# A pair's split queries and keys go to their matmul operands by way of DRAM, and two-block pieces are transposed in one transfer

## The chip, the cores and the metric

The kernel runs on one core of one Trainium2 chip. The metric is the device time of one execution in microseconds, median of the runs shown. The core has five engines with an instruction stream each: TensorE (PE, with its weight loads as PEld), VectorE (DVE), ScalarE (ACT), GpSimd (POOL) and SyncE (SP). In this kernel SP issues every DMA; its rows are marked SPq. Each stream runs in order: an instruction that waits holds up everything behind it on its engine.

## The reference

Attention with a decay bias, and behind it a two-layer network with an ELU in the middle, all in 32-bit floats:

```
scores = (q @ k.T) / sqrt(64)                     # 8 batches x 8 heads, 576 x 576, head size 64
cum    = cumsum(max(s, 0))                        # along the sequence
scores = where(causal, -1e9, scores + min(cum[key] - cum[query], 0))
attn   = exp(scores - rowmax);  attn /= rowsum + 1e-9
x      = attn @ v                                 # 4608 tokens x 512
h      = x @ w_in                                 # 512 -> 2048
out    = where(h > 0, h, exp(min(h, 0)) - 1) @ w_out   # 2048 -> 512
```

## The kernel before

**Work.** A "pair" is two heads of one batch; a "piece" is a batch with a range of its 128-query blocks. Three kinds of piece come in this order: batches 0 to 2 with blocks 0 and 1 ("low", computed in 32 bits, 12 units); then batch 3 with blocks 0 and 1 and batches 4 to 7 whole (20 pairs, named with `_None` in the profile because their preparation hangs on a unit without a head number); then blocks 2 and 3 of batches 0 to 3 (16 "late" pairs). The 18 chunks of 256 tokens of the network follow the pieces and fill TensorE between the attention steps.

**A pair's operands.** Outside the low stage every 32-bit number is split into two 16-bit floats, a high and a low part, and products are sums of 16-bit matmuls. `prepare_pair` loads a pair's keys (`stk`) and queries (`stq`), two transfers for keys and two or four for queries, the first head in partitions 0 to 63 and the second in 64 to 127. It takes their largest value (`peak`, L601 and L604), makes a scale from it (`pk`, L939 to L941), and splits them into `kp` and `qp` (L408 to L410 high, L960 or L956 and L957 low). Then `spread` copies the parts into the operand tile `set`, where both heads lie side by side and a column holds 64 numbers of one part above 64 of another: two transfers (one a head) for each of the six places `kh`, `kh2`, `qh`, `qh2`, `kl`, `ql`, so twelve, and a thirteenth brings the decay rows (`set<-aux_dram`). There are two sets, used in turn. Then come the scores (L1040), the masked minimum (L1043), the exponential (L1048).

**Weights times values.** `halved` scales a block's exponentials and splits them into `p16` tiles (L1093, L1095 or L1097 high, L1101 or L1087 and L1088 low); one DMA transpose per block (`turned_load`, L389) brings them into `T`; `weighing` multiplies by the values (L1209) when all transposes of both heads are there, and the result goes to `x_dram`. For a late pair both heads use the same two `p16` tiles, so that the second head's splitting waits until the first head's transposes have read them. The first 64 queries of a pair are one small extra unit (`psh_None`, `tr_None`, `vs_None`); its 64 value rows have a transfer of their own (`stv`), into one of the three `st` buffers that the keys and queries use as well.

**Network.** `load_x` loads a chunk (`xc<-x_dram`), one transfer per 128 channels and row range; then come the split (`xh`, `xl`), the first layer (L1383), the ELU (L1395 to L1422) and the second layer (L1440).

**Order.** No order is written by hand. `Plan` gets every step with an estimated cost per engine that could do it, and places, one by one, the step that can start first (then the one of highest priority) on its engine's stream. A plain transfer costs SP 430 ns in it (`SP_COST`), a transpose 1250 ns, and data are taken to land 1800 ns (`LAG`) plus bytes / 225 (`RATE`) after their turn in the transfer queue. The resulting order is fixed; at run time each engine only waits for semaphores.

Of the kernel before, what the change touches and what calls it, by code (L numbers as in the profile page):

```python
# [17 lines left out]
P = 128  # L18
# [9 lines left out]
N_ST, N_A, N_AV, N_H, N_IO, N_G, N_X, N_T, N_V = 3, 2, 1, 3, 3, 1, 1, 2, 4  # L28
# [17 lines left out]
SP_COST = 430.0  # L46
# [12 lines left out]
class Buf:  # L59
# [15 lines left out]
    @property  # L75
    def v(self):
        if self.tile is None:
            self.tile = self.make()
        return self.tile

# [5 lines left out]
class Plan:  # L86
# [41 lines left out]
    def op(self, prio, ways, reads=(), writes=(), late=()):  # L128
# [5 lines left out]
        for accesses, write in ((reads, False), (writes, True)):  # L134
            for a in accesses:
                b, part = a if isinstance(a, tuple) else (a, None)
                if not b.parts and b not in o.bufs:

                    o.new.append((b, self.place(b)))
                    b.first = o  # L140
# [195 lines left out]
def kernel(  # L336
# [46 lines left out]
    def load(prio, dst, src, reads, writes, nbytes, late=(), lag=LAG):  # L383
        return op(prio, [("SP", SP_COST, lambda: nc.sync.dma_start(dst(), src()), lag, nbytes)],  # L384
                  reads, writes, late)

    def turned_load(prio, units, dst, src, reads, writes):

        op(prio, [("SP", 1250.0, lambda: nc.sync.dma_start_transpose(dst(), src()), LAG,  # L389
                   units * P * P * 2)], reads, writes)  # L390
# [119 lines left out]
    Q1, Q2, K1, K2 = range(4)  # L510
# [61 lines left out]
    pair_sets = [plan.buf(const, [P, 4, 2, S], F16, "set_0")]  # L572

# [6 lines left out]
    all_tops = [plan.buf(const, [P, P], F32, f"tops_{m}") for m in range(3)]  # L580
# [11 lines left out]
    junk = const.tile([P, 2 * (NQ + 1) * D], BF16, name="junk")  # L592
# [22 lines left out]
    def scales_of(prio, spans, dst):  # L615

        n = len(spans)
        kind = 1 if dst == 0 else 2 * (dst >= C_LOW)
# [119 lines left out]

    def prepare_low(u):
# [4 lines left out]
        u.q = plan.buf(sb, [P, 2 * LOW], F32, f"ql_{u.tag}", tag="qs", bufs=2)  # L744
# [23 lines left out]
    def scoring_low(u):  # L768
        prio = u.prio
        sm = plan.buf(sb, [P, 1 + 2 * CUT], F32, f"sml_{u.tag}", tag="sm", bufs=2)  # L770
        u.first = plan.buf(sb, [P, P], F32, f"pl_{u.tag}", tag=("khs", "vs0")[u.turn])
        u.pp = {}
        tiles = [(u.first, P)]
# [9 lines left out]
        def block(i, h):  # L783
            n = 1 + 2 * i + h
            place = i + CUT * u.turn
            if h == 0:
                pt = pp[place]
            else:
                pt = plan.buf(sb, [P, pd[i]], F32, f"pl{n}_{u.tag}", tag=f"p16_{place}")
# [81 lines left out]
    def group_values(u):  # L871
# [4 lines left out]
        nv = 2 * (u.last + 2)  # L876
        whole = nv - 2 * (u.last < NQ - 1)
        va = plan.buf(sb, [P, NP, nv, D], F32, f"va_{at}", tag=home.key[1])
        for j in range(NP):
            load(prio + j, lambda j=j: va.v[:, j, :whole], lambda j=j: vb[u.b, j, :, 1 : 1 + whole], [],  # L880
                 [(va, (j, "whole"))], P * whole * D * 4)
            for rows in HALF[: nv - whole]:
                load(prio + j, lambda j=j, rows=rows: va.v[rows, j, whole:], lambda j=j: vb[u.b, j, :HB, 1 + whole : 1 + nv],
                     [], [(va, (j, rows.start))], HB * 2 * D * 4)
# [6 lines left out]
        return va, col  # L891

    def pair_values(u, va, col):
# [4 lines left out]
        src = lambda: va.v[:, u.j].rearrange("p (n h) d -> p h n d", h=2)  # L898
# [16 lines left out]
    def prepare_pair(u, o):  # L915
# [6 lines left out]
        kp, qp = (plan.buf(sb, [P, 2, S], F16, f"{m}p_{u.tag}", tag="qs", bufs=2) for m in "kq")  # L922
        for m, rows in enumerate(HALF):
            load(prio, lambda m=m, rows=rows: sk.v[rows, :n], lambda m=m: kT[b, :HB, 2 * j + m, :n], [], [(sk, m)],
                 HB * n * 4)
        for m, rows in enumerate(HALF):
            if c0:
                at = (1 - m) * (w - HB)
                load(prio, lambda rows=rows, at=at: sq.v[rows, at : at + HB],
                     lambda m=m: qT[b, j, :HB, m * HB : (m + 1) * HB], [], [(sq, (m, 0))], HB * HB * 4)  # L930
            load(prio, lambda m=m, rows=rows: sq.v[rows, m * c0 : m * c0 + nb * P].rearrange("d (i t) -> d i t", t=P),
                 lambda m=m: qT[b, j, :HB, P:].rearrange("d (i m t) -> d i m t", m=2, t=P)[
                     :, u.blocks[0] : u.last + 1, m], [], [(sq, (m, 1))], HB * P * nb * 4)
# [15 lines left out]
        def split(m, size, t, src):  # L949

            high, low = (lambda: t.v[:, 0, :size]), (lambda: t.v[:, 1, :size])
            x = lambda: src.v[:, :size]
            scaled(prio, size, high, x, lambda: by(m), [src, (pk, 2)], [(t, 0)])
# [9 lines left out]
            ], [(pk, 2), (t, 0)], [src, (t, 1)])  # L963
# [20 lines left out]
        load(prio, lambda: o.v[HB : HB + 3, K2, :, :n],  # L984
             lambda: aux_dram.v[b * H + 2 * j : b * H + 2 * j + 2, :, :n].rearrange("h m t -> m h t"),
             [aux_dram], [(o, "aux")], n * 12)
        spread(kp, 1, n, top, K2, "kl")
        spread(qp, 1, w, low, Q1, "ql")
# [3 lines left out]
    def prepare(u):  # L992
# [14 lines left out]
        u.vs = plan.buf(sb, [P, 1, 2, D], F32R, f"vs_{u.tag}", tag="vs0")  # L1007
        v_src = lambda: vb[b, j, :, 0:1]
        sv = st_buf(f"stv_{u.tag}")

        def v3():
            return sv.v[:, :D].rearrange("p (n d) -> p n d", d=D)
# [3 lines left out]
        rest(prio, D, lambda: u.vs.v[:, :1, 1], v3,  # L1016
             lambda: u.vs.v[:, :1, 0].bitcast(F32), [sv], [u.vs])
# [51 lines left out]
    def halved(u, i, pt, sm, col):  # L1069

        r, prio = slice(col, col + 1), u.prio
        k, turns = (pw[i] + HB * (i < u.last)) // P, u.turns[i]
        t16 = plan.buf(sb, [P, turns * P], F16, f"p16_{u.tag}_{i}", tag=f"p16_{i + u.step}")

        def whole(t, m):
            v = t.v[:, P:] if i == u.last else t.v
            return v.rearrange("p (k m q) -> p k m q", m=2, q=P)[:, :, m]

        def rest(t, m):
            return t.v[:, m * HB : (m + 1) * HB]  # L1080
# [5 lines left out]
        def scaled_rest(part):  # L1086
            pool.tensor_scalar(own(part), own(part), sm.v[:, r], 1.0, ALU.mult, ALU.mult)  # L1087
            pool.tensor_tensor(part(t16, 1), own(part), part(t16, 0), ALU.subtract)  # L1088

        for part, n in ((whole, k * P), (rest, HB))[: 1 + (i == u.last)]:  # L1090
            high, low = (part, 0), (part, 1)
            op(prio, [
                ("Pool", 160 + 1.04 * n, lambda part=part: pool.tensor_scalar(  # L1093
                    part(t16, 0), own(part), sm.v[:, r], 1.0, ALU.mult, ALU.mult)),
                ("DVE-SB", 220 + 0.7 * n, lambda part=part: dve.tensor_scalar(  # L1095
                    part(t16, 0), own(part), sm.v[:, r], None, ALU.mult)),
                ("ACT", 295 + n / 1.2, lambda part=part: act.activation(  # L1097
                    part(t16, 0), own(part), AF.Copy, scale=sm.v[:, r])),
            ], [sm, (pt, "data"), (pt, "pad")], [(t16, high)])
            op(prio, [  # L1100
                ("DVE-SB", dve_2(n), lambda part=part: dve.scalar_tensor_tensor(  # L1101
                    part(t16, 1), own(part), sm.v[:, r], part(t16, 0), ALU.mult, ALU.subtract)),
                ("Pool", pool_1(n) + pool_2(n), lambda part=part: scaled_rest(part)),
            ], [sm, (pt, "pad"), (t16, high)], [(t16, low), (pt, "data")])
# [504 lines left out]
```

## Time and profile before

| what | value |
|---|---|
| time, median of 3 runs | 1146.38 us (1142.46 to 1148.72) |
| the profiled execution, its own time | 1142.85 us |
| its span, first to last instruction | 1141.0 us |
| mean granted TensorE clock | 0.976 |
| PE / DVE / ACT / POOL busy | 1035.0 / 842.7 / 676.5 / 262.0 us |
| DMA queue, share of 16 engines' span | 58.9% |
| transfers into `set` from `kp` and `qp` | 432 |
| DMA transposes | 208 |

"Busy" counts an engine's own work, so SP, which only issues, has no such number; the length of an issue stands in the rows of its line and in the timeline. A wait row says which engine and line stood idle, what ended the idle time, the sum, the times, and the longest. The profile's stretches here are the low stage and its passage (0 to 150 us), the 20 pairs (about 150 to 750), the 16 late pairs (about 750 to 1050), and a tail of network alone.

### The profile page before, as it was taken

The page shows a single profiled execution, that of the slowest core. Times are in us where ns is not written, and L with a number is a line of the kernel's source. Part 1 is how long each engine was busy: PE and PEld are TensorE (multiplying, and loading weights), DVE is VectorE, ACT ScalarE, POOL GpSimd, SP SyncE. Part 2 cuts the span into 40 slices and gives each one's busy share as a digit, 9 for nine tenths or more (in the row PEclk, how much of TensorE's full clock was granted, in tenths as well). Part 3 has the DMA queues.
Part 4 walks back from the last instruction along what each step waited for, and adds up shares of the span by engine and source line. Part 5 has one row for each costly group of instructions (what it writes and reads, how often), then busy time and mean ns, then how long its engine had stood idle before and what let it go on. Part 6 is the DMA issues. An engine that isn't in the chain of part 4 may idle for free.

```text
span 1141.0 us, 22403 instructions
## 1 busy us (share of the span) xinstructions
PE 1035.0 (91%) x7299; PEld 695.8 (61%) x7299; DVE 842.7 (74%) x2361; ACT 676.5 (59%) x1579; POOL 262.0 (23%) x442
## 2 busy tenths in 40 slices
PE   7999998799899688989899998898999899899998
PEld 6676565566556456656566665565666566566665
DVE  7997997558778687878688876777788687776332
ACT  5887755456556565656566665565566565546343
POOL 6331442121322222222232222111122112200000
PEclk9999999999999889999899999999999999999999
DMA  7897224345656686667666866575575675655200
GB/s 194 270 276 227 58 89 86 94 101 164 142 137 132 154 190 139 125 147 165 142 151 136 194 130 155 118 182 125 134 181 127 135 160 137 140 123 102 50 20 19
DMA packets 304665, 158.41 MB, mean 139 GB/s; under 512 B 218356, under 2 KB 286692, under 8 KB 304548
## 3 DMA queue, kind: packets, MB, share of 16 engines
q1 hardware_dynamic: 304548, 156.98, 58.9%
q8 instruction: 58, 0.95, 0.4%
q14 instruction: 59, 0.48, 0.1%
HBM read 62.80 MB, written 19.24 MB: 72 GB/s over the span
## 4 chain that ended last, share of the span: by engine, by line
PE 35%; DVE 10%; DMA 8%; SPq 6%; issue 4%; ACT 3%; POOL 0%; DVEq 0%; ACTq 0%; POOLq 0%
PE h L1383 15%; PE o L1440 13%; SPq L384 5%; PE sc L1040 3%; PE av L1209 3%; DMA T<-p 2%; DMA stq<-in_qT_dram 2%; DMA x_dram<-x_None 2%; DVE p L1043 2%; DVE p L1101 2%; SPq L389 1%; DVE h L1415 1%; ACT g L1395 1%; DMA va<-in_vb_dram 1%; DMA stq_None<-in_qT_dram 1%
## 5 line engine op out<-in xcount | busy, mean ns | idle before, releaser
L1383 PE MATMUL h<-xh,wp 128*128 128x256 f16 x2176 | 408.3, 276 | 2.5 <-DVE gg L1422 1.7
L1440 PE MATMUL o<-wp,gg 128*128 128x512 f16 x1632 | 398.2, 383 | 4.7 <-DVE gg L1422 2.9
L1383 PEld LDWEIGHTS <-wp 128*128 128x128 f16 x3264 | 321.5, 99 | 74.9 <-issue 3.6
L1383 PE MATMUL h<-xl,wp 128*128 128x256 f16 x1088 | 300.6, 276 | 0.9 <-DVE xl L1359 0.8
L1440 PEld LDWEIGHTS <-gg 128*128 128x128 f16 x1632 | 158.6, 99 | 155.5 <-DVE gg L1422 6.8
L1101 DVE SCALAR_TENSOR_TENSOR p<-p,sm,p 128x512 f16<-128x512 f32 (+3 forms) x268 | 159.1, 618 | 28.7 <-ACT p L1097 24.1
L1048 ACT ACTIVATE p<-p,mn 128x192 f32<-128x192 f32 (+1 forms) x232 | 143.6, 619 | 39.3 <-DVE mn L1043 37.8
L1415 DVE SCALAR_TENSOR_TENSOR h<-g,cs,h 128x512 f32<-128x512 f32 x136 | 102.0, 750 | 55.5 <-ACT g L1402 53.8
L1395 ACT ACTIVATE g<-h,cs 128x512 f32<-128x512 f32 x136 | 92.6, 681 | 82.8 <-PE h L1383 82.5
L1093 POOL TENSOR_SCALAR p<-p,sm 128x512 f16<-128x512 f32 (+3 forms) x96 | 63.9, 670 | 335.5 <-DMA T<-p 113.2
L1040 PE MATMUL sc<-set 128*128 128x288 f16 (+3 forms) x544 | 114.2, 303 | 28.2 <-DVE mn L1043 26.1
L1043 DVE CUSTOM_DVE_ANT_0 p<-sc,maskw 128x192 f32<-128x192 f32 (+1 forms) x232 | 109.3, 480 | 21.4 <-PE sc L1040 17.2
L1419 ACT ACTIVATE gg<-h 128x512 f16<-128x512 f32 x129 | 76.5, 593 | 73.0 <-DVE h L1415 68.4
L1097 ACT ACTIVATE p<-p,sm 128x512 f16<-128x512 f32 (+3 forms) x148 | 82.8, 574 | 53.3 <-DMA T<-p 32.7
L1422 DVE SCALAR_TENSOR_TENSOR gg<-h,gg 128x512 f16<-128x512 f32 x136 | 93.1, 684 | 18.0 <-ACT gg L1419 17.4
L1040 PEld LDWEIGHTS <-set 128*128 128x128 f16 x584 | 55.3, 99 | 77.6 <-issue 40.6
L1209 PE MATMUL av<-T,v 128*64 128x256 f16 (+5 forms) x960 | 69.8, 288 | 28.0 <-DMA T<-p 26.1
L1209 PEld LDWEIGHTS <-v 128*64 128x64 f16 x960 | 53.0, 114 | 52.4 <-issue 23.9
L1402 ACT ACTIVATE g<-g 128x512 f32<-128x512 f32 x80 | 50.2, 628 | 2.1
L408 POOL TENSOR_SCALAR v<-va,scales 128x320 f16<-128x320 f32 (+1 forms) x42 | 23.6, 565 | 92.0 <-PE av L1209 89.3
L1048 ACT ACTIVATION_READ_ACCUMULATOR p<-p,mn 128x1 f32 x232 | 43.7, 188 | 0.0
L1406 DVE TENSOR_SCALAR g<-g 128x512 f32<-128x512 f32 x64 | 28.1, 439 | 19.2 <-ACT g L1395 18.9
(196 smaller groups left out, 1237.7 us busy)
## 6 DMA issues: line engine op xcount, KB each, us to landing
va<-in_vb_dram SPq DMA_DIRECT2D x32, 320.0 KB
raws<-in_w_in_dram SPq DMA_DIRECT2D x16, 512.0 KB
raws<-in_w_out_dram SPq DMA_DIRECT2D x16, 512.0 KB
out_dram<-ost SPq DMA_DIRECT2D x32, 256.0 KB
set<-kp_None SPq DMA_DIRECT2D x96, 72.0 KB
set<-qp_None SPq DMA_DIRECT2D x96, 72.0 KB
set<-kp SPq DMA_DIRECT2D x96, 72.0 KB
xc<-x_dram SPq DMA_DIRECT2D x44, 128.0 KB
```

What stands on the lines that cost most here:

```text
L1040: pe_.matmul(view(sc.v[:, :cw]), l, r, start=n == 0, stop=n == len(pairs) - 1)
L1043: op(prio, [("DVE", 84 + dve_p(cw), lambda i=i, sc=sc: dve.tensor_tensor_reduce(pt.v[:, i * cw : (i + 1) * cw], sc.v[:, :cw], mv(i * cw, c ...
L1048: op(prio, [("ACT", 480 + w / 1.2, lambda: act.activation(pt.v[:, :w], pt.v[:, :w], AF.Exp, bias=mn.v[:, n - 1 : n], scale=-1.0, accum_out ...
L1097: ("ACT", 295 + n / 1.2, lambda part=part: act.activation(part(t16, 0), own(part), AF.Copy, scale=sm.v[:, r])),
L1101: ("DVE-SB", dve_2(n), lambda part=part: dve.scalar_tensor_tensor(part(t16, 1), own(part), sm.v[:, r], part(t16, 0), ALU.mult, ALU.subtract)),
L1209: pe_.matmul(av.v[w.h * HB : (w.h + 1) * HB, dst], w.values.v[:, w.h, kb, v], part(w, kb, m), start=kb == 0 and m == 0 and v == 0, stop=kb ...
L1383: pe_.matmul(columns(k), weight_part(f, 0, part)[1]()[:, c * P : (c + 1) * P], xx.v[:, c], start=(c == 0 and m == 0), stop=(c == NCB - 1 a ...
L1395: op(side, [("ACT", act_c(W) + (0 if native else 90), lambda: act.activation(g.v, hp.v, AF.Exp, scale=1.0 if native else by(3)))], [hp] + ...
L1415: op(side, [("DVE", dve_p(W), lambda: dve.scalar_tensor_tensor(hp.v, g.v, by(2 if sign[0] else 1), hp.v, ALU.mult, ALU.max))], [g, cs], [hp])
L1419: ("ACT", act_c(W), lambda: act.activation(gg.v[:, 0], hp.v, AF.Copy, scale=2.0**-DOWN)),
L1422: op(side, [("DVE", dve_p(W), lambda: dve.scalar_tensor_tensor(gg.v[:, 1], hp.v, 2.0**-DOWN, gg.v[:, 0], ALU.mult, ALU.subtract))], [hp, ( ...
L1440: pe_.matmul(acc[i].v, gg.v[:, g, at], weight_part(f, 1, part)[1](), start=(f == 0 and m == 0), stop=(f == NF - 1 and m == 2),)
```

## The change

Both parts of queries and keys are written into one tile `parts` (rows: low queries, high queries, high keys, low keys). Two transfers per pair (one a head; four for a late pair, whose queries are shorter than its keys) write them to a DRAM tile `spread`, one for each set. Three transfers then read `spread` into the set: three rows at once into the upper half (`top`), two rows into the lower half (`low`), and the high queries once more (`q2`). The set's rows are reordered (`Q1, K1, K2, Q2`) so that a transfer reads and writes adjoining rows, and both heads' columns are taken in one run.

A late pair's and batch 3's two blocks of a head share one `p16` tile and one transpose of 17 (or 9) units instead of two of 8 and 9 (4 and 5); the two heads have a tile each. In whole pieces two blocks share a tile, with a transpose each as before. The 64 extra value rows come with the group's values (`va`, one more slot per pair) and the transfer `stv` is gone, so `st` has two users per pair. `load_x` loads two times 128 channels in one transfer. The low units' queries and second-head tiles get other places in memory. In `Plan`, a plain transfer costs SP 460 ns, one of the pair's 600 ns, a transpose 1320 ns.

```diff
-N_ST, N_A, N_AV, N_H, N_IO, N_G, N_X, N_T, N_V = 3, 2, 1, 3, 3, 1, 1, 2, 4
+N_ST, N_A, N_AV, N_H, N_IO, N_G, N_X, N_T, N_V, N_PARTS = 3, 2, 1, 3, 3, 1, 1, 2, 4, 1
...
-SP_COST = 430.0
+SP_COST, SP_SHORT, SP_TURN = 460.0, 600.0, 1320.0
...
-    Q1, Q2, K1, K2 = range(4)
+    Q1, K1, K2, Q2 = range(4)
+    QL, QH, KH, KL = range(4)
...
+    spreads = [plan.buf(dram, [HB, 4, 2, S], F16, f"spread_{k}") for k in range(2)]
...
-        kp, qp = (plan.buf(sb, [P, 2, S], F16, f"{m}p_{u.tag}", tag="qs", bufs=2) for m in "kq")
+        parts = plan.buf(sb, [P, 4, S], F16, f"parts_{u.tag}", tag="parts", bufs=N_PARTS)
+        spread = spreads[pair_sets.index(o)]
...
-        split(1, n, kp, sk)
-        split(0, w, qp, sq)
-        u.w, first = w, (S - w, S)
-
-        def spread(src, part, size, rows, m, label):
-
-            for h, own in enumerate(HALF):
-                def dst(h=h):
-                    if m in (K1, K2):
-                        return o.v[rows, m, h, :size]
-                    return o.v[rows, m].rearrange("p h t -> p (h t)")[:, first[h] : first[h] + size]
-
-                load(prio, dst, lambda own=own: src.v[own, part, :size], [(src, part)], [(o, (label, h))], HB * size * 2)
+        split(1, n, KH, KL, sk)
+        split(0, w, QH, QL, sq)
+        u.first = S - w if c0 else 0
+        for h, rows in enumerate(HALF):
+            at = u.first * (1 - h)
+            for m0, m1, size in ((QL, KL + 1, w),) if n == w else ((QL, KH, w), (KH, KL + 1, n)):
+                load(prio, lambda h=h, at=at, m0=m0, m1=m1, size=size: spread.v[:, m0:m1, h, at : at + size],
+                     lambda rows=rows, m0=m0, m1=m1, size=size: parts.v[rows, m0:m1, :size],
+                     [(parts, m) for m in range(m0, m1)], [(spread, (h, m0))], HB * (m1 - m0) * size * 2, cost=SP_SHORT)
+        span = slice(u.first, S + n)
+
+        def flat(v):
+            return v.rearrange("p m h t -> p m (h t)")[:, :, span]
 
         top, low = HALF
-        spread(kp, 0, n, top, K1, "kh")
-        spread(kp, 0, n, low, K1, "kh2")
-        spread(qp, 0, w, top, Q1, "qh")
-        spread(qp, 0, w, top, Q2, "qh2")
...
-        spread(kp, 1, n, top, K2, "kl")
-        spread(qp, 1, w, low, Q1, "ql")
+        load(prio, lambda: flat(o.v[top, Q1 : K2 + 1]), lambda: flat(spread.v[:, QH : KL + 1]),
+             [spread], [(o, "top")], HB * 6 * S * 2, cost=SP_SHORT)
+        load(prio, lambda: flat(o.v[low, Q1 : K1 + 1]), lambda: flat(spread.v[:, QL : KH + 1 : 2]),
+             [spread], [(o, "low")], HB * 4 * S * 2, cost=SP_SHORT)
+        load(prio, lambda: flat(o.v[top, Q2 : Q2 + 1]), lambda: flat(spread.v[:, QH : QH + 1]),
+             [spread], [(o, "q2")], HB * 2 * S * 2, cost=SP_SHORT)
...
-        load(prio, v3, v_src, [], [sv], P * D * 4)
-        rounded(prio, D, lambda: u.vs.v[:, :1, 0], v3, [sv], [u.vs])
...
+        src, used = (lambda: u.va.v[:, j, :1]), values_of(u.va, j)
+        rounded(prio, D, lambda: u.vs.v[:, :1, 0], src, used, [u.vs])
...
-        t16 = plan.buf(sb, [P, turns * P], F16, f"p16_{u.tag}_{i}", tag=f"p16_{i + u.step}")
...
+        joint, at = n == CUT, (i - u.blocks[0] + 1) % n
+        if (i - u.blocks[0]) % CUT == 0:
+            units = 2 * u.turns[i + 1] - 1 if joint else turns + u.turns[i + 1]
+            u.t16 = plan.buf(sb, [P, units * P], F16, f"p16_{u.tag}_{i}", tag=f"p16_{CUT * (u.h if joint else i // CUT)}")
...
-        turned_load(prio, turns, lambda: u.pt.v[:, at :: u.n_blocks][:, :turns], lambda: t16.v, [t16], [(u.pt, i)])
+        if joint and i < u.last:
+            return
...
+        if joint:
+            turned_load(prio, 2 * turns - 1, lambda: u.pt.v, lambda: t16.v, used, [u.pt])
+        else:
+            turned_load(prio, turns, lambda: u.pt.v[:, at::n][:, :turns],
+                        lambda: t16.v[:, base * P : (base + turns) * P], used, [(u.pt, i)])
...
-        for c in range(NCB):
+        for m in range(2):
...
-                load(-1000 + ch, lambda c=c, t=t, n=n: xc[c // 2].v[:, c % 2, t : t + n],
-                     lambda c=c, b=b, r=r, n=n: x_dram.v[b, c, :, r : r + n],
-                     [(x_dram, (b, c, late))], [(xc[c // 2], (c, t))], P * n * 4)
+                load(-1000 + ch, lambda m=m, t=t, n=n: xc[m].v[:, :, t : t + n],
+                     lambda m=m, b=b, r=r, n=n: x_dram.v[b, 2 * m : 2 * m + 2, :, r : r + n].rearrange("c p n -> p c n"),
+                     [(x_dram, (b, c, late)) for c in (2 * m, 2 * m + 1)], [(xc[m], t)], 2 * P * n * 4)
```

More of the change, by code (lines that the diff above doesn't have):

```diff
@@ L79, in v, with __init__ @@
         return self.tile
+class Piece:
+    def __init__(self, whole, label, view):
+        self.whole, self.label, self.view = whole, label, view
+    @property
+    def v(self):
+        return self.view(self.whole.v)
 class Op:
@@ L134, in op @@
         for accesses, write in ((reads, False), (writes, True)):
+            expanded = []
             for a in accesses:
                 b, part = a if isinstance(a, tuple) else (a, None)
+                if not isinstance(b, Piece):
+                    expanded.append((b, part))
+                elif part is None:
+                    known = [key for key in b.whole.parts if key is not None and key[0] == b.label]
+                    expanded += [(b.whole, key) for key in known or [(b.label, None)]]
+                else:
+                    expanded.append((b.whole, (b.label, part)))
+            for b, part in expanded:
                 if not b.parts and b not in o.bufs:
@@ L788, in block @@
             else:
[L789 removed]
+                start = sum(pd[:i])
+                pt = Piece(u.both, i, lambda t: t[:, start : start + pd[i]])
             u.pp[h, i] = pt
@@ L1087, in scaled_rest @@
             pool.tensor_scalar(own(part), own(part), sm.v[:, r], 1.0, ALU.mult, ALU.mult)
-            pool.tensor_tensor(part(t16, 1), own(part), part(t16, 0), ALU.subtract)
-        for part, n in ((whole, k * P), (rest, HB))[: 1 + (i == u.last)]:
-            high, low = (part, 0), (part, 1)
+            pool.tensor_tensor(part(1), own(part), part(0), ALU.subtract)
+        for part, size, label in ((whole, k * P, "whole"), (rest, HB, "rest"))[: 1 + (i == u.last)]:
+            high, low = ((t16, (i, label, m)) for m in range(2))
@@ L1092, in halved @@
             op(prio, [
[L1093 to L1099, printed above, removed]
@@ L1100, in halved @@
-            op(prio, [
[L1101 to L1104, printed above, removed]
-        at = (i - u.blocks[0] + 1) % u.n_blocks
-        turned_load(prio, turns, lambda: u.pt.v[:, at :: u.n_blocks][:, :turns], lambda: t16.v, [t16], [(u.pt, i)])
+                ("Pool", 160 + 1.04 * size, lambda part=part: pool.tensor_scalar(
+                    part(0), own(part), sm.v[:, r], 1.0, ALU.mult, ALU.mult)),
@@ new lines, in halved @@
+                ("DVE-SB", 220 + 0.7 * size, lambda part=part: dve.tensor_scalar(
+                    part(0), own(part), sm.v[:, r], None, ALU.mult)),
+                ("ACT", 295 + size / 1.2, lambda part=part: act.activation(
+                    part(0), own(part), AF.Copy, scale=sm.v[:, r])),
+            ], [sm, (pt, "data"), (pt, "pad")], [high])
+            op(prio, [
+                ("DVE-SB", dve_2(size), lambda part=part: dve.scalar_tensor_tensor(
+                    part(1), own(part), sm.v[:, r], part(0), ALU.mult, ALU.subtract)),
+                ("Pool", pool_1(size) + pool_2(size), lambda part=part: scaled_rest(part)),
+            ], [sm, (pt, "pad"), high], [low, (pt, "data")])
@@ new lines, in halved @@
+        if joint and i < u.last:
+            return
+        used = [
+            (t16, (b, label, m)) for b in (u.blocks if joint else [i])
+            for label in ("whole", "rest")[: 1 + (b == u.last)] for m in range(2)]
+        if joint:
+            turned_load(prio, 2 * turns - 1, lambda: u.pt.v, lambda: t16.v, used, [u.pt])
+        else:
+            turned_load(prio, turns, lambda: u.pt.v[:, at::n][:, :turns],
+                        lambda: t16.v[:, base * P : (base + turns) * P], used, [(u.pt, i)])
@@ L1119, in scoring, with row @@
         o = u.set
-        used = [(o, part) for part in (
-            "aux", "weights", *((part, h) for part in ("kh", "kh2", "qh", "qh2", "kl", "ql") for h in (0, 1)))]
+        def row(m, at, size):
+            return o.v[:, m].rearrange("p h t -> p (h t)")[:, at : at + size]
+        used = [(o, part) for part in ("top", "low", "q2", "aux", "weights")]
         if u.h is None:
@@ L1143, in block @@
             n = i - u.blocks[0]
-            first = (S - u.w, S + c0)[u.h] + n * P
+            first, keys = (u.first, S + c0)[u.h] + n * P, (u.first, S)[u.h]
             if u.step and i < u.last:
@@ L1149, in block @@
                 lambda at, w: maskw.v[:, max(WM - pw[i] + at, 0) :][:, :w], used,
-                lambda at, w: [(
-                    o.v[:, q].rearrange("p h t -> p (h t)")[:, first : first + P], o.v[:, k, u.h, at : at + w]) for q, k in ((Q1, K1), (Q2, K2))],
+                lambda at, w: [(row(q, first, P), row(k, keys + at, w)) for q, k in ((Q1, K1), (Q2, K2))],
                 (sm, n, i == u.last, u.n_blocks, UP),
```

90 lines of the change are left out of this document (49 added, 41 removed).

## The prediction, written before the changed kernel was run

> **What bounds the kernel now.** I read the page's head and chain first, then the clock, then each engine by stretch (PE, PEld, DVE, ACT, POOL busy, clock, DMA share, GB/s), then what TensorE waits for, and last the transfers.
>
> ```profile
> span 1141.0 us, 22403 instructions
> PE 1035.0 (91%) x7299; PEld 695.8 (61%) x7299; DVE 842.7 (74%) x2361; ACT 676.5 (59%) x1579; POOL 262.0 (23%) x442
> ```
> ```profile
> core 0: 1141.0 us, clock 0.976
> ```
> ```profile
> 150.00:750.00 600.00, 535.24 (x3843) 355.33 (x3842) 458.62 (x1315) 351.00 (x834) 156.84 (x232) 0.97 0.61 138
> 750.00:1050.00 300.00, 272.80 (x2079) 185.12 (x2077) 224.81 (x600) 173.33 (x360) 49.63 (x81) 0.98 0.63 139
> 1050.00:1141.00 91.00, 87.01 (x612) 58.15 (x609) 29.83 (x50) 36.70 (x61) 0.00 (x0) 1.00 0.16 38
> ```
>
> TensorE is busy for 1035 of 1141 us, so this change, which takes no matmul away, can win only idle time and clock. Idle are 600 - 535.2 = 65 us in the stretch of the 20 pairs and 300 - 272.8 = 27 us in that of the late pairs: 92 us that the change can touch. The clock of 0.976 costs at most 0.024 x 1141 = 27 us more. What ends TensorE's idle times (the waits of PE alone):
>
> ```profile
> PE sc L1040 <- DVE mn L1043: 26.8, 27, 3.5
> PE av L1209 <- DMA T<-p: 26.1, 13, 4.9
> PE tr_None L1175 <- POOL psh_None L1061: 8.6, 3, 4.0
> PE tr_None L1175 <- ACT psh_None L1065: 7.0, 4, 3.0
> PE sc_None L1040 <- DVE mn L1043: 4.6, 2, 3.5
> PE sc_None L1040 <- DMA set<-qp_None: 4.5, 4, 1.7
> ```
>
> So 30.6 us wait for a transfer directly (26.1 + 4.5), and 47.0 us for DVE, POOL or ACT (26.8 + 8.6 + 7.0 + 4.6). Why these are late shows in the two lines that issue transfers. Columns: shortest / median / longest issue in ns; below, who waited, in us and times. First the plain transfers:
>
> ```profile
> L384 SPq DMA_DIRECT2D set<-kp_None x120: 461/587/1562, 121.7 to 681.3; - x120
> L384 SPq DMA_DIRECT2D set<-qp_None x120: 467/594/1818, 124.8 to 682.9; - x120
> L384 SPq DMA_DIRECT2D set<-kp x96: 461/587/1493, 694.5 to 1024.5; - x96
> L384 SPq DMA_DIRECT2D set<-qp x96: 467/595/1177, 697.5 to 1025.8; - x96
> L384 SPq DMA_DIRECT2D xc<-x_dram x92: 320/440/1086, 29.8 to 1067.2; - x92
> ...
> L384 SPq DMA_DIRECT2D stv_None<-in_vb_dram x20: 328/366/2000, 121.3 to 668.3; - x20
> ...
> L384 SPq DMA_DIRECT2D stq<-in_qT_dram x32: 615/648/1771, 684.8 to 1013.0; - x32
> ...
>   ACT junk L604: 73.1, 36
> ```
>
> Then the transposes:
>
> ```profile
> L389 SPq DMA_TRANSPOSE T<-p x208: 1188/1258/3864, 175.1 to 1057.8; - x104
> ...
>   POOL p L1093: 113.2, 16
>   ACT p L1097: 32.7, 20
> ```
>
> ACT takes a pair's peak (L604) and stands still for the queries' landing 73 us in all; POOL and ACT stand still for transposes that have not yet read a `p16` tile. An issue of a `set` transfer takes 0.59 us where the planner reckons 0.43, so SP falls behind the planned order. A stretch of SP's timeline among the late pairs:
>
> ```profile
> 949.22 1.23 SPq L384 DMA_DIRECT2D set<-kp  x2
> 950.50 1.24 SPq L384 DMA_DIRECT2D set<-qp  x2
> 951.77 2.46 SPq L384 DMA_DIRECT2D stq<-in_qT_dram  x2
> 954.28 1.24 SPq L384 DMA_DIRECT2D stk<-in_kT_dram  x2
> 955.62 1.26 SPq L389 DMA_TRANSPOSE T<-p  x1
> 956.98 0.52 SPq L384 DMA_DIRECT2D x_dram<-x  x1
> 957.60 1.30 SPq L389 DMA_TRANSPOSE T<-p  x1
> ```
>
> From 949.22 to 958.90 (9.68 us) SP issues for 9.25 us, and a transpose goes out only after four `set` and four load issues. SP is the serial queue on which a pair's landings and its transposes line up. So I read the kernel as bound by TensorE, with stalls of which a part comes from a full SP.
>
> **The change part by part.** *SP's time.* Removed: 432 `set` issues, 120 x 0.587 + 120 x 0.594 + 96 x 0.587 + 96 x 0.595 = 255 us; 20 `stv`, 20 x 0.366 = 7 us; 48 of the `xc` and first-chunk loads (two for four), 48 x 0.44 = 21 us. Added: five transfers for each of 20 pairs and seven for each of 16, 212. None like them is in the trace. Below, one costs as the shortest `set` issue, 0.46 us, sum 98 us; above, as the longest, 1.82 us, sum 386 us; I take the late `stq` row, whose transfers also move two runs per partition, 0.648 us, sum 137 us, because every short issue lies around it. Transposes: 40 fewer of 1.258 us, 50 us, if a 17-unit one costs no more than a 9-unit one, nothing if its cost grows with the units; shortest and median of units 4 to 9 differ by 6%, so I take 45. Net: 255 + 7 + 21 + 45 - 137 = 191 us of SP's time fewer (from 328 fewer to 103 more).
>
> *The path of one pair.* Before, a full pair's split is followed by 12 x 0.59 = 7.1 us of issues and one landing. After: 2 x 0.65, a landing in DRAM, 3 x 0.65, a landing. Landing pieces from the chain of waits, in order of time:
>
> ```profile
> 594.30 2.21 DMA x_dram<-x_None
> ...
> 848.90 1.90 DMA set<-qp
> ...
> 969.18 3.41 DMA T<-p
> ```
>
> With 2.21 us for the write to DRAM: before 7.1 + 1.9 = 9.0 us, after 1.3 + 2.2 + 1.95 + 1.9 = 7.35 us. For a late pair (four writes) it is 8.65 us. So the extra hop is paid by the issues saved. The new wait is the three reads' for the writes, on SP: behind it stand transposes, stores and `xc` loads, and DVE, ACT and POOL wait for those. The planner puts the reads after its own landing time, 1.8 us plus 295 KB / 225 = 3.1 us, more than the 2.2 us seen, and fills the gap with other issues; without that cover it is 36 x 2.2 = 79 us of SP's time, still below the 191.
>
> The Trainium skill speaks against this part: by the page "DMA: Bandwidth & Descriptors", section "Latency and other measured facts", the roughly 2 us that any transfer costs is mostly the round trip of the write receipt, and DRAM (HBM) is the slowest target, up to 2 us under load. The store row agrees in size; paid in full by 36 pairs, an estimate by the page gives 72 us of landing against the 36 x 5 issues saved, and the sum would lose its gain if the hop could not be covered.
>
> *The joint transpose.* Late pairs and batch 3 only. The data part of a landing is 3.41 - 1.90 = 1.5 us for about 9 units; 17 units make it 2.85, so 1.35 us later, against one issue of 1.26 us fewer ahead of it. Bounds for the 16 late pairs: a whole further landing each, 16 x 3.41 = 55 us worse, and, since each head now has its own tile and POOL and ACT need not wait for the first head's transposes, 10 us better (the share of the 26.1 us that I would give this at most). Value: 4 us worse.
>
> *Where SP's relief arrives.* Waits for `set`, 4.5 us, gone but for a rest: -4 (0 to -4.5). TensorE's wait for transposes, 26.1 us: half, since some of it is late DVE and ACT work ahead of the transpose and not SP: -13 (0 to -26). The 47.0 us of late DVE, POOL and ACT: these wait for each other as well, so a fifth: -9 (0 to -23). Clock: 27 us lost, of which the same share goes as of idle time, 22 of 92: -6 (0 to -13).
>
> The skill's page "TensorE: Matmul & The Clock Gate", section "Part 1: The HAM clock gate", gives half rate only after an idle window of about 3.4 us; the longest waits above reach 3.5 to 4.9 us, so by it only removing these few wins clock, and the sum without the term would be -22.
>
> *At nothing:* the peak over one more slot of values (64 columns in 20 pairs, on ACT or DVE, which are idle 41% and 26%); the wider `p16` tiles of whole pieces (a later reuse, hidden by POOL's 77% idle); two writes of 64 x 4 x 576 x 2 bytes = 295 KB more per pair, on DMA engines 61% busy (without that slack, each landing grows). The `st` buffer freed by `stv` lets the next keys load earlier and helps the same waits.
>
> Sum: -4 - 13 - 9 + 4 - 6 = -28 us. From the profiled execution's own 1142.85 us (span 1141.0 and 1.85 around it) this gives 1114.9. The median shown, 1146.38, lies 3.5 above that execution, so I forecast 1118 us.
>
> **Rivals.** *Nothing comes of it, about 1145 us.* TensorE's waits are set by DVE (busy 458.6 of 600 us, 76%): then `sc <- mn` stays at 26.8 us, the transposes' wait is only renamed, and only the 4.5 us for `set` go, against 4 for the joint transposes. For: DVE heads the waits, and SP itself waits for DVE's low parts before transposes. Against: 73 us of ACT's waits hang on landings alone.
>
> *SP sets far more, about 1092 us.* If all direct waits go (-30.6), half of the 47.0 (-23) and the clock follows (27 x 54 / 92 = -16), with the joint transposes at +4 and one more stall in place of the old ones at +12, 1142.85 - 54 = 1089, median 1092. For: SP's timeline above is full. Against: many engines are late at once, and one being freed seldom frees all.
>
> *The joint transpose makes it slower, about 1167 us.* Place: `av <- T` in the late stretch. If the heads' products there come right behind their transposes, every one of 16 pairs waits for the longer landing, at 2.4 us (midway from 1.35 to 3.41): +38; of the other terms' -26 two thirds (600 of 900 us) are won elsewhere, -17. 1142.85 + 21 = 1164, median 1167. It decides from 26 / 16 = 1.6 us per pair on. For: `av <- T` is already TensorE's second wait. Against: one issue fewer stands before it.
>
> *It doesn't do what it says:* if a new issue costs 1.8 us, SP gains nothing; that goes with the first and third rival.
>
> **How the numbers follow.** Forecast 46% (own range 1104 to 1134), nothing 18%, far more 18%, slower 18%. About 0.5% (5.7 us) is what a measurement of this kernel can tell from no change. Faster: 46 + 18 + 2 (the edge of "nothing") = 66%; within 16%; slower 18%. All lower ends together (-4.5 - 26 - 23 - 10 - 13) would give 1070, which needs every stall to go; the range starts at 1085, takes in "far more" and "nothing", ends at 1154, and leaves out most of the slower case.
>
> **What would show it.** Right: 168 transposes and 212 `spread` and `set` transfers but for the decay rows, with medians of 0.55 to 0.75 us; ACT's wait for landings (73 us) halved; TensorE idle below 75 us from 150 to 1050 (or its shorter equivalent); clock above 0.98. Wrong: issues of the new transfers above 1.2 us; `av <- T` above 30 us in the late stretch; new waits of TensorE for `set`; SP waiting for `spread`. The forecast fails as a whole if DVE's share of TensorE's waits grows by what the transfers' share loses.

## The result, and the profile after

The changed kernel takes 1036.96 us, median of 4 runs (1034.60 to 1038.93), against 1145.32 (1142.46 to 1148.72) for the kernel before: a ratio of 0.905, 95% interval 0.902 to 0.908. The forecast was 1118 with a range from 1085: right in direction, with a quarter of the gain. The profiled execution took 1034.6 us.

The page's head, and the clock of the core:

```profile
span 1032.8 us, 21782 instructions
PE 1003.1 (97%) x7305; PEld 688.7 (67%) x7305; DVE 845.2 (82%) x2346; ACT 669.0 (65%) x1559; POOL 295.9 (29%) x487
```
```profile
core 0: 1032.8 us, clock 0.996
```

TensorE's idle time fell from 106 us (1141.0 - 1035.0) to 30 (1032.8 - 1003.1), and its busy time by 32 us though its matmuls are the same. By an estimate from the clock rows, 23 of these 32 are the clock's: 0.024 x 1141 = 27 us lost before, 0.004 x 1033 = 4 now. The stretches now end earlier; they are, in order, the 20 pairs, the late pairs and the network's tail (PE, PEld, DVE, ACT, POOL busy, clock, DMA share, GB/s):

```profile
150.00:640.00 490.00, 480.96 (x3615) 328.24 (x3614) 435.85 (x1256) 335.70 (x802) 159.21 (x240) 1.00 0.86 186
640.00:925.00 285.00, 279.84 (x2195) 191.77 (x2193) 242.46 (x642) 181.32 (x380) 71.15 (x111) 1.00 0.87 193
925.00:1032.80 107.80, 103.86 (x727) 69.32 (x724) 32.95 (x48) 42.01 (x67) 0.00 (x0) 1.00 0.08 24
```

In the attention stretch TensorE is idle 14 us (9.0 + 5.2), where it was 92. The DMA engines are busier (0.86 where they were 0.61). The waits of PE, to be held against those of before:

```profile
PE sc L1065 <- DVE mn L1068: 5.7, 12, 1.0
...
PE av L1252 <- DMA T<-p: 2.8, 3, 1.8
PE tr_None L1218 <- ACT psh_None L1090: 2.1, 1, 2.1
...
PE tr_None L1218 <- POOL psh_None L1086: 1.5, 2, 0.8
```

Every kind of wait that was listed before fell, those for DVE, ACT and POOL (47.0 to 9.3 us) as much as those for transfers. On SP, the plain issues and who waited for them:

```profile
L404 SPq DMA_DIRECT2D set<-spread x108: 451/592/1801, 120.0 to 889.6; - x108
...
L404 SPq DMA_DIRECT2D spread<-parts x64: 574/616/1530, 594.4 to 883.4; - x64
L404 SPq DMA_DIRECT2D xc<-x_dram x46: 370/493/1145, 45.4 to 949.4; - x46
...
L404 SPq DMA_DIRECT2D spread<-parts_None x40: 540/589/1285, 114.2 to 577.2; - x40
...
  ACT junk L626: 25.6, 24
```

and the transposes with theirs:

```profile
L409 SPq DMA_TRANSPOSE T<-p x168: 1206/1309/4601, 172.6 to 922.4; - x168
...
  POOL p L1125: 27.5, 6
...
  PE av L1252: 2.8, 3
```

A stretch of SP's timeline among the late pairs:

```profile
815.03 2.66 SPq L404 DMA_DIRECT2D spread<-parts  x4
817.73 1.29 SPq L404 DMA_DIRECT2D stq<-in_qT_dram  x2
819.07 1.24 SPq L404 DMA_DIRECT2D stk<-in_kT_dram  x2
820.48 2.57 SPq L409 DMA_TRANSPOSE T<-p  x1
823.14 0.47 SPq L404 DMA_DIRECT2D set<-aux_dram  x1
823.72 2.42 SPq L404 DMA_DIRECT2D set<-spread  x3
826.30 3.70 SPq L409 DMA_TRANSPOSE T<-p  x1
```

A joint transpose occupies SP for 2.57 and 3.70 us here, where a transpose of before took 1.26 to 1.30.

### The profile page after: what moved, and what is told of

Its sections match the earlier page's. It is cut to its first block, busy times and chain, and to the rows that moved or that the text cites. A ratio compares the mean times of both kernels' runs of the same rounds, so it can differ in the third digit from the quotient of the medians.

```text
span 1032.8 us, 21782 instructions
## 1 busy us (share of the span) xinstructions
PE 1003.1 (97%) x7305; PEld 688.7 (67%) x7305; DVE 845.2 (82%) x2346; ACT 669.0 (65%) x1559; POOL 295.9 (29%) x487
## 5 line engine op out<-in xcount | busy, mean ns | idle before, releaser
L1427 PE MATMUL h<-xh,wp 128*128 128x256 f16 x2176 | 402.7, 273 | 0.7 <-DVE gg L1466 0.7
L1484 PE MATMUL o<-wp,gg 128*128 128x512 f16 x1632 | 392.7, 380 | 0.5 <-DVE gg L1466 0.5
L1427 PEld LDWEIGHTS <-wp 128*128 128x128 f16 x3264 | 317.4, 98 | 69.7 <-issue 2.1
L1427 PE MATMUL h<-xl,wp 128*128 128x256 f16 x1088 | 297.3, 273 | 1.1 <-DVE xl L1403 1.1
L1133 DVE SCALAR_TENSOR_TENSOR p<-p,sm,p 128x512 f16<-128x512 f32 (+3 forms) x257 | 162.8, 662 | 4.9 <-POOL p L1125 2.4
L1129 ACT ACTIVATE p<-p,sm 128x512 f16<-128x512 f32 (+3 forms) x139 | 75.1, 557 | 19.0 <-DVE sm L1079 5.5
L1252 PE MATMUL av<-T,v 128*64 128x256 f16 (+5 forms) x960 | 62.4, 278 | 2.8 <-DMA T<-p 2.8
L1252 PEld LDWEIGHTS <-v 128*64 128x64 f16 x960 | 48.5, 110 | 23.3 <-issue 12.3
L428 POOL TENSOR_SCALAR v<-va,scales 128x320 f16<-128x320 f32 (+1 forms) x45 | 26.8, 599 | 64.9 <-PE av L1252 58.3
L1068 DVE CUSTOM_DVE_ANT_0 p<-sc,maskw,mn 128x288 f32<-128x288 f32 x64 | 32.9, 514 | 7.1 <-PE sc L1065 5.5
```

What stands on the lines that cost most here:

```text
L1068: op(prio, [("DVE", 84 + dve_p(cw), lambda i=i, sc=sc: dve.tensor_tensor_reduce(pt.v[:, i * cw : (i + 1) * cw], sc.v[:, :cw], mv(i * cw, c ...
L1129: ("ACT", 295 + size / 1.2, lambda part=part: act.activation(part(0), own(part), AF.Copy, scale=sm.v[:, r])),
L1133: ("DVE-SB", dve_2(size), lambda part=part: dve.scalar_tensor_tensor(part(1), own(part), sm.v[:, r], part(0), ALU.mult, ALU.subtract)),
L1252: pe_.matmul(av.v[w.h * HB : (w.h + 1) * HB, dst], w.values.v[:, w.h, kb, v], part(w, kb, m), start=kb == 0 and m == 0 and v == 0, stop=kb ...
L1427: pe_.matmul(columns(k), weight_part(f, 0, part)[1]()[:, c * P : (c + 1) * P], xx.v[:, c], start=(c == 0 and m == 0), stop=(c == NCB - 1 a ...
L1484: pe_.matmul(acc[i].v, gg.v[:, g, at], weight_part(f, 1, part)[1](), start=(f == 0 and m == 0), stop=(f == NF - 1 and m == 2),)
```

## The experiments

Adding up the durations of all SP transfers of a trace gives a number that no view shows: **SP's issue time**, 833 us before and 694 after. Between the first and the last transpose SP issues for 741 of 885 us before (0.84) and for 615 of 752 after (0.82). The theories were: **A**, SP's issues are the throughput limit of the attention stretch; **B**, the planned order came true because the planner now counts SP's issues at what they take; **C**, a pair's path or its buffers matter, not the issues. Times are medians; each ratio stands against the kernel before, run beside it.

| run | time us | ratio (95%) | SP issue us | PE idle us |
|---|---|---|---|---|
| before | 1145.3 | 1 | 833 | 106 |
| after | 1037.0 | 0.905 (0.902 to 0.908) | 694 | 30 |
| e1 before, new planner costs | 1126.7 | 0.984 (0.981 to 0.987) | 832 | 91 |
| e2 after, old planner costs | 1041.0 | 0.909 (0.906 to 0.913) | 702 | 33 |
| e3 after, twelve direct transfers | 1091.9 | 0.954 (0.951 to 0.956) | 792 | 66 |
| e4 before, by way of DRAM | 1070.1 | 0.935 (0.932 to 0.938) | 744 | 50 |
| e5 after, six idle transfers a pair | 1122.1 | 0.979 (0.976 to 0.982) | 829 | 85 |
| e6 before, half of set on ACT's queue | 1091.2 | 0.952 (0.949 to 0.956) | 713, ACT 122 | 65 |
| e7 after, separate transposes | 1036.7 | 0.905 (0.902 to 0.908) | 701 | 28 |
| e8 after, key and query loads on ACT's queue | 1042.6 | 0.910 (0.906 to 0.913) | 573, ACT 112 | 33 |
| e9 after, three idle transfers a pair | 1071.9 | 0.936 (0.934 to 0.939) | 769 | 56 |
| e10 as e5, unplanned | 1129.1 | 0.987 (0.984 to 0.990) | 824 | 98 |
| e11 after, stv in st | 1059.8 | 0.926 (0.924 to 0.928) | 710 | 47 |
| e12 after, four xc loads | 1049.4 | 0.918 (0.916 to 0.920) | 717 | 38 |
| e13 after, stv in a buffer of its own | 1038.2 | 0.906 (0.903 to 0.909) | 697 | 30 |
| e14 before, stv in a buffer of its own | 1142.7 | 0.998 (0.996 to 1.000) | 833 | 102 |
| e15 after, two st buffers | 1037.2 | 0.904 (0.900 to 0.908) | 700 | 31 |
| e16 after, separate transposes, one tile for both heads | 1032.9 | 0.902 (0.899 to 0.905) | 688 | 26 |
| e17 after, again | 1038.9 | 0.907 (0.905 to 0.908) | 696 | 33 |
| e18 e16 again | 1032.6 | 0.901 (0.900 to 0.903) | 687 | 26 |

Every edit also gives the planner another order to find, and no edited run holds the order fixed. In e1 the order alone moves the time by 20 us with SP's issue time unchanged, so a difference of that size in a single row can be the order's; the larger ones, and rows that agree, carry the argument.

**Is it the planner's costs? e1 and e2.** The costs put into the kernel before, and taken out of the changed one:

```diff
-SP_COST = 430.0
+SP_COST, SP_SHORT, SP_TURN = 460.0, 600.0, 1320.0
```
```diff
-SP_COST, SP_SHORT, SP_TURN = 460.0, 600.0, 1320.0
+SP_COST, SP_SHORT, SP_TURN = 430.0, 430.0, 1250.0
```

> The kernel before with only the planner's three costs for SP changed (460 ns for a plain transfer, 600 for the pair's, 1320 for a transpose); no transfer is removed. Theory A (SP's time: the stalls went because SP has fewer issues to make): stays within 15 us of 1145, since SP still issues for about 830 us. Theory B (truth of the plan: the stalls went because the planned order now counts SP's issues at what they take): most of the gain is here, 1040 to 1080. Theory C (what frees buffers and shortens the pair's path): 1135 to 1150.

> The changed kernel with the planner's old SP costs (430, 430, 1250), all transfers as changed. Theory A: 1030 to 1050, the transfers are still few. Theory B: the gain is mostly lost, 1100 to 1140, with TensorE waiting for DVE and transposes again. Theory C: 1035 to 1050.

Truer costs win 20 us in the kernel before (1146.5 beside it, to 1126.7), which A's expectation (within 15 us of 1145) missed by some 3 us, and about 4 us in the changed one, where the intervals overlap. B holds for a fifth of the gain at most.

**Is it the way by DRAM? e3 and e4.** Undone in the one, done alone in the other (e4 writes `kp` and `qp` with four transfers, so seven a pair; old costs):

```diff
-        load(prio, lambda: flat(o.v[top, Q1 : K2 + 1]), lambda: flat(spread.v[:, QH : KL + 1]), ...
+        direct(top, K1, KH, n, "kh")
+        direct(low, K1, KH, n, "kh2")
+        direct(top, Q1, QH, w, "qh")
+        direct(top, Q2, QH, w, "qh2")
+        direct(top, K2, KL, n, "kl")
+        direct(low, Q1, QL, w, "ql")
```
```diff
-        spread(kp, 0, n, top, K1, "kh")
...
+        for t, m0, size in ((kp, KH, n), (qp, QL, w)):
+            for h, rows in enumerate(HALF):
+                at = u.first * (1 - h)
+                load(prio, lambda h=h, at=at, m0=m0, size=size: spread.v[:, m0 : m0 + 2, h, at : at + size],
+                     lambda t=t, rows=rows, size=size: t.v[rows, :, :size], [t], [(spread, (h, m0))], ...)
```

> The changed kernel with the set filled straight from the parts tile by twelve transfers, without DRAM; costs, joint transposes, values and chunk loads as changed. SP issues 220 transfers more (about 130 us of issue). Theory A: gives back most of the gain, 1090 to 1130. Theory B: the plan knows of the issues, so it gives back what SP's time costs in the plan, little: 1040 to 1065. Theory C: 1040 to 1060.

> The kernel before with only the way by way of DRAM (seven transfers a pair in place of twelve, 180 fewer in all, old planner costs). Theory A: more than half of the gain, 1060 to 1100. Theory B: little, 1110 to 1140, since the plan still undercounts each issue. Theory C: 1120 to 1145.

Undoing it loses 55 us; doing it alone wins 75 of the 108 us, though the transposes, the buffers on the chip and the planner's costs are those of before and the queue moves more bytes (178 MB against 157). In e4's waits of PE those for DVE fell with the rest, and the wait for `set` did not grow by the extra hop (4.5 us before):

```profile
PE av L1215 <- DMA T<-p: 10.2, 10, 1.7
PE sc L1043 <- DVE mn L1046: 5.6, 10, 1.0
PE sc_None L1043 <- DMA set<-spread: 4.9, 6, 1.9
```

**Is it SP's issues or the pair's path? e5, e9 and e10.** Transfers whose data nobody reads are added (six or three a pair), in e10 with the planner counting them at 1 ns:

```diff
+        for m in (QL, QH, KH, KL, QH, KH):      # e9: (QL, KH, KL)
+            r0 = idle_n[0] * HB
+            idle_n[0] += 1
+            load(prio, lambda r0=r0: idle_dram[r0 : r0 + HB], lambda: maskw.v[:HB, :32], [(parts, m), maskw], [], HB * 64, cost=SP_SHORT)
```

> The changed kernel with six small transfers a pair added (64 rows of 64 bytes from a constant tile to an unused DRAM tile, 216 in all, planned at 600 ns each); they carry nothing that anyone waits for. Theory A (SP's issues are the throughput limit of the attention stretch): SP issues some 110 to 130 us more, and 0.6 to 0.8 of that comes back as time, 1100 to 1140 or, since TensorE hides the first part, at least 1080. Theory C (what matters is the pair's path or the bytes): unchanged, 1035 to 1050.

> The changed kernel with three small idle transfers a pair, 108 in all, half the dose of six a pair (which cost 85 us). Theory A in its simple form (every us of SP's issues comes back at 0.65): 1037 + 42 = 1079. Theory A with a bend (TensorE is the limit until SP's issues exceed what fits beside it): less than half of 85, 1045 to 1070. A cost of each extra landing and not of the issue: also half, 1079, so this run cannot tell that apart; it tells the bend.

> The same six idle transfers a pair, but the planner counts them at 1 ns, so its order is that of the changed kernel but for the idle issues put in. Theory A: the same 1115 to 1135 as planned. Theory B (truth of the plan): clearly worse than the planned ones, 1140 to 1180.

Of e5's trace, the idle transfers and the first PE waits:

```profile
L404 SPq DMA_DIRECT2D idle_dram<-maskw x216: 445/595/1953, 111.8 to 1010.7; - x108
```
```profile
PE sc L1071 <- DVE mn L1074: 23.0, 26, 4.2
PE av L1258 <- DMA T<-p: 15.1, 11, 3.4
```

Idle issues bring back 85 of the 108 us, and with them the two waits that headed the list of before, with the wait for DVE in front. C's expectation, 1035 to 1050, is out: nothing reads these transfers, and they add 0.9 MB to the 178.5 MB on the queue. In the plan each also reads `parts`, so that the next pair's split waits for it; the trace puts 3.4 us of idle time down to them in all. The dose bends: 75 us of issue time cost 35 us (e9, 2 us above the 1045 to 1070 expected for a bend), the next 60 cost 50. The same transfers unplanned cost 7 us more than planned. Nor is their order that of the changed kernel, though the expectation says so: ACT has 1577 instructions, not 1559, and POOL 458, not 487. So idle issues lose time in three different orders.

**The issues on another queue: e6 and e8.**

```diff
-                load(prio, dst, lambda own=own: src.v[own, part, :size], [(src, part)], [(o, (label, h))], HB * size * 2)
+                (act_load if h else load)(prio, dst, lambda own=own: src.v[own, part, :size], [(src, part)], [(o, (label, h))], HB * size * 2)
```
```diff
-            load(prio, lambda m=m, rows=rows: sk.v[rows, :n], ...
+            other_load(prio, lambda m=m, rows=rows: sk.v[rows, :n], ...
```

> The kernel before with all twelve transfers into the set kept, but the second head's six issued on ScalarE's queue (216 in all, planned at 600 ns there), old costs elsewhere. Theory A: SP issues about 128 us less, and the time falls to 1050 to 1085, though nothing goes by way of DRAM and ACT gets the issues. Theory C (the route, fewer transfers): 1130 to 1160, or slower by ACT's load.

> The changed kernel with the loads of a pair's keys and queries (184 transfers) issued on ScalarE's queue, planned at 600 ns there. Theory A with TensorE 97% busy as the new bound: SP's relief of about 125 us wins nothing more, and ACT's load costs a little: 1025 to 1050. If SP were still the limit after the change: below 1015.

In e6 every transfer of before is kept and none goes by way of DRAM; half of the set's issues leave SP, the bytes stay the same (143.8 MB on SP's queue and 13.2 on ACT's, 157.0 before), and 54 us are won. Two of its rows:

```profile
L388 ACTq DMA_DIRECT2D set<-kp_None x60: 468/470/1809, 122.0 to 649.8; - x60
L384 SPq DMA_DIRECT2D set<-kp_None x60: 461/546/1473, 122.1 to 652.3; - x60
```

The expectation (1050 to 1085) was missed by 6 us, and TensorE is still idle for 65 us; that ACT pays for its 122 us of issues is likely, but not shown. Whether the time on SP's stream counts or a transfer's turn in the queue behind it, no run separates: both left SP here. In e8 SP is relieved of 121 us more than the change does, ACT takes 112 us of issues, and nothing is won: after the change TensorE, 97% busy, is the limit.

**The other parts: e7, e11 to e16.** Separate transposes with a tile a head (e7); the value rows by a transfer of their own into `st` (e11) or into a small buffer (e13, and e14 for the kernel before); four `xc` loads (e12, the old loop); two `st` buffers (e15); separate transposes and one tile for both heads of a late pair (e16):

```diff
-        joint, at = n == CUT, (i - u.blocks[0] + 1) % n
+        joint, at, own_tile = False, (i - u.blocks[0] + 1) % n, n == CUT      # e7; e16: no tile per head in late pairs
```
```diff
-        src, used = (lambda: u.va.v[:, j, :1]), values_of(u.va, j)
+        sv = st_buf(f"stv_{u.tag}")      # e13, e14: plan.buf(sb, [P, D], F32, ..., tag="stv_own")
+        src, used = (lambda: sv.v[:, :D].rearrange("p (n d) -> p n d", d=D)), [sv]
+        load(prio, src, lambda: vb[b, j, :, 0:1], [], used, P * D * 4)
```
```diff
-N_ST, ... = 3, 2, 1, 3, 3, 1, 1, 2, 4, 1
+N_ST, ... = 2, 2, 1, 3, 3, 1, 1, 2, 4, 1      # e15
```

> The changed kernel with a transpose for each block of a two-block piece again (40 transposes more), the two heads still with a tile each. Theory A: about 40 x 1.26 = 50 us of SP's time more, of which 15 to 40 us come back as time, 1050 to 1075. My prediction's term for the joint transpose (4 us worse than separate ones, without SP's share): 1030 to 1036.

> The changed kernel with the pair's 64 value rows loaded by a transfer of their own into an st buffer again (20 transfers more). Theory A: 20 x 0.37 = 7 us of SP, at most 5 us of time, 1037 to 1043. Theory C (the st buffer that comes free for the next keys is what matters): 1045 to 1070.

> The changed kernel with a chunk's loads one per 128 channels again (48 transfers more). Theory A: 48 x 0.44 = 21 us of SP, 5 to 15 us of time, 1040 to 1052. If TensorE hides the first of SP's issues: 1036 to 1041.

> The changed kernel with the 64 value rows loaded by a transfer of their own (20 more), into a small buffer of their own, so that st keeps two users a pair. If the 23 us of the run with st came from the buffer (Theory C): 1035 to 1043. If they came from the issues (Theory A): 1052 to 1062.

> The kernel before with only that: stv in a small buffer of its own, every transfer kept. Theory A: SP's issues are unchanged, so 1138 to 1148. Theory C: the next keys and queries are loaded a pair earlier, 1110 to 1130.

> The changed kernel with two st buffers in place of three (no transfer more). Theory A: 1035 to 1045. Theory C: loss of the third buffer costs as much as stv in it did, 1055 to 1065.

> The changed kernel with separate transposes and, in late pairs, one p16 tile for both heads as before, so that the second head's splitting waits for the first head's transposes. Separate transposes alone cost nothing. If the tile per head matters: 1045 to 1060, with POOL and ACT waiting for T again in the late stretch. If not: 1034 to 1042.

The old `xc` loads cost 12 us and 23 us of SP's time (e12), as A expected, though another order can do as much. The joint transpose carries nothing: e7's 208 transposes occupy SP for 293 us, the changed kernel's 168 for 288, because one of 17 units takes about as long as two of 8 and 9, or longer. Here A's expectation of 1050 to 1075 failed for the size of its term, not its sense: there was no SP time to lose. With stv in `st` 23 us are lost (e11), with the same transfers in a buffer of their own nothing measurable (e13): so not the issues. Nor is it the third buffer, whose loss alone costs nothing (e15); and in the kernel before, taking stv out of `st` wins 0.2%, interval to 1.000 (e14). In e11's trace POOL stands still for the landing of `stv` for 82.1 us (18 times), in e13's for 7.4 us (2 times), so the rows come late when they wait for an `st` buffer; how this becomes 23 us of TensorE's time is not settled.

**A faster version: e17 and e18**, the changed kernel and e16 side by side.

> The changed kernel itself, beside the next one on one chip, for a difference of less than half a per cent: 1034 to 1040.

> The changed kernel with separate transposes and one p16 tile for both heads of a late pair. If the joint transpose, whose issue takes 3.1 us, is a small loss: 1030 to 1035 and below the changed kernel by 2 to 5 us. If the lower time of the earlier run was its chip: no difference.

0.901 (0.900 to 0.903) against 0.907 (0.905 to 0.908): without the joint transpose and the tile per head the kernel is 6 us faster still (2 to 5 were expected). POOL then waits for transposes again, and TensorE does not:

```profile
L409 SPq DMA_TRANSPOSE T<-p x208: 1206/1270/2652, 174.4 to 970.0; - x104
...
  POOL p L1125: 69.4, 9
...
  PE av L1252: 0.8, 2
```

e16 had come out at 1032.9 before, 1 us below the range expected if the tile does not matter. Since e7 (a tile a head, separate) is no faster than the changed kernel, the 6 us hang on the tile per head, or on the order that the planner finds without it; which, was not tried.

## Why the prediction was wrong

**What bounds the kernel.** "Bound by TensorE, with stalls of which a part comes from a full SP" was half of it. SP's issues were not a contribution to some stalls but set the pace of the attention stretch: between the first and the last transpose they fell by 126 us (741 to 615), and that stretch became 133 us shorter (885 to 752). The tail of network behind the last transpose grew from 83 to 110 us, which takes 27 of them back. The prediction saw 9.25 of 9.68 us full in one place and did not add the issues up over the stretch.

**SP's time.** Forecast 191 us fewer, measured 139 (833 - 694). The new issues were sized well: 137 forecast; 108 x 0.592 + 64 x 0.616 + 40 x 0.589 = 127 by the medians above, 134 by adding up the durations. The transposes were not: 45 us saved in the forecast, 6 us more in the traces (281 before, 288 after). The premise that the issue hardly depends on the units was taken from rows of 4 to 9 units. Two of its sums are off without touching the forecast: "328 fewer" leaves out the new issues, and with 98 us for them it is 230; and "36 x 5" issues saved are 20 x 7 + 16 x 5 = 220.

**Where SP's relief arrives** is the step that failed. Its terms against the rows: waits for `set` -4, measured gone (-4.5); waits for transposes -13, measured -23 (26.1 to 2.8); DVE, POOL and ACT -9, measured -38 (47.0 to 9.3); clock -6, measured -23 (the estimate above). The third is the large miss. Together the measured terms make 88 of the 108 us; some 10 of the rest are waits that the rows above leave out, and 9 are busy time of TensorE that the clock does not account for. "These wait for each other as well, so a fifth" treats the engine named in a wait as its cause. e5 shows the contrary: with nothing but idle issues added on SP, TensorE's wait for DVE rises from 5.7 to 23.0 us. SP's queue at its limit was seen in the waits of all that hang on it. The clock mostly went with the waits: 0.996 after, 0.972 in e5. It does not follow their sum alone: e1 has less idle time than before (91 us) and a lower clock (0.965), with single waits of up to 12.6 us.

The page "TensorE: Matmul & The Clock Gate" of the Trainium skill, section "Part 1: The HAM clock gate", has half rate come after an idle window of some 3.4 us. As a limit on the single wait, which is how the prediction used it, the traces do not bear it out: the granted clock went to 0.50 behind 2.5 us almost without a matmul before the change, and behind 2.1 us after it (columns as in the stretches above, the clock third from the end; first the kernel before, then the changed one).

```profile
340.50:343.00 2.50, 0.00 (x0) 0.00 (x0) 2.47 (x8) 0.47 (x1) 0.00 (x0) 1.00 0.90 168
343.00:346.40 3.40, 3.39 (x13) 1.85 (x13) 2.54 (x11) 1.79 (x7) 0.75 (x1) 0.50 0.81 103
```
```profile
152.95:155.05 2.10, 0.01 (x1) 0.01 (x2) 2.07 (x8) 0.47 (x2) 0.48 (x1) 1.00 0.47 145
155.10:158.50 3.40, 3.40 (x16) 2.43 (x17) 3.28 (x13) 2.92 (x5) 2.81 (x4) 0.50 0.51 162
```

In the trace before, half rate adds up to 55 us, in the one after to 7. The sum by that rule, -22, was no nearer, since it lacked the same waits.

**The path of a pair.** The extra hop cost almost nothing that shows: e4 waits 4.9 us for `set` where 4.5 were before, and SP's wait for the writes shows once, with 1.2 us. These three entries are all of SP's waits that name the new transfers:

```profile
SPq L409 <- DMA set<-spread: 4.0, 7, 1.4
...
SPq L404 <- DMA set<-spread: 3.7, 7, 0.8
...
SPq L404 <- DMA spread<-parts_None: 1.2, 1, 1.2
```

So the landing in DRAM was hidden but for that. The write receipt, which the Trainium skill makes most of a transfer's fixed 2 us (page "DMA: Bandwidth & Descriptors", section "Latency and other measured facts"), decided nothing here.

The same page of the Trainium skill, section "Issuing engines are not separate DMA queues", says that the sequencer's time to initiate a DMA "is usually small relative to the DMA itself". In this kernel that time was the limit, and moving a part of it off SP bought 54 us (e6).

**The joint transpose.** +4 us forecast; the joint transpose itself 0 (e7 took 1036.7, where the term put it at 1030 to 1036), with the tile per head +6 (e18 against e17). The sign came out by luck: the reason given, a longer landing, is not shown, and the joint transpose alone costs nothing. Of the marks set for a right forecast all came out (168 transposes, 212 transfers at 589 to 616 ns, ACT's wait for landings from 73 to 26 us, clock above 0.98): they tested whether stalls and issues fall, not by how much. The sign for failure as a whole, DVE's share of the waits growing by what the transfers' share loses, could not tell either: DVE's share of the listed waits rose from 40 to 47% and the transfers' fell from 39 to 23%, while in us both fell.

**At nothing.** Stv and the `st` buffer were put down as help for the same waits; e11 shows 23 us for stv in `st` once SP is relieved. The `xc` loads, in SP's sum only, show 12.

**The rivals.** "Far more" (1092) was the nearest. Its mechanism is the one that the runs show; it stopped at half of the DVE waits and added 12 us of a new stall, and neither was so. Its "against", that one engine freed seldom frees all, did not hold here. "Nothing comes of it" took DVE for the limit; DVE does the same work after (845 us) in 108 us less. "The joint transpose makes it slower" needed `av <- T` to grow, and it fell to 2.8 us; "It doesn't do what it says" needed issues of 1.8 us, and they take 0.6.

## What to carry to other kernels

Add up the issue times of the engine that issues transfers, over the stretch in question: no busy row shows them. The share alone does not decide: 0.84 of the stretch was the limit before, and 0.82 after is none, since TensorE is 97% busy and more relief wins nothing (e8). A cheap test is to add idle transfers and see the time and the waits come back, under whatever names the waits stand. One us of issues was worth between 0.45 and 0.84 us here (54 for 120 in e6, 75 for 89 in e4; the whole change 108 for 139).

## What the runs showed of the hardware

A transpose of 17 units takes SP 1.9 to 2.4 times as long to issue as one of 8 or 9. The transposes of the changed kernel from 700 us on, all joint, shortest / median / longest in ns:

```profile
L409 SPq DMA_TRANSPOSE T<-p x27: 1961/3095/4601, 700.7 to 922.4; - x27
```

against a median of 1280 before, from 750 us on, for 8 and 9 units. In e3, where the DMA engines are busy for 0.66 of the late stretch in place of 0.87, the joint ones take 2468 ns from 770 us on, about two of the small; what the difference hangs on was not tried. A transfer of 64 rows costs SP about 0.6 us whether a row is 64 bytes (595 ns, e5), 1152 bytes (`set<-kp_None` of whole pairs, 587 ns) or, for most pairs, 2304 to 6912 bytes (`set<-spread`, 592 ns); on ACT's queue the transfer that took SP 546 ns took 470 (e6). And the kernel ran faster with more bytes moved: 178 MB on the queue against 157.
